# A gated attention and GLU kernel: output weight loads moved behind the h stores of their half, moments of tiles 8 to 11 split in two pairs

## The chip, the cores and the metric

The kernel runs on one core of a Trainium2 chip. The metric is the device time of one execution in microseconds (us); the time before is the median of three runs, 751.63 us (749.72 to 752.89). The five instruction streams are called PE (matrix products; its weight loads are PEld), DVE (vector), ACT (scalar), POOL (GpSimd) and SP (here it only issues DMAs). Each stream runs its instructions strictly in the order in which the program emitted them, and waits on semaphores for the others.

## The reference

With x of 2048 rows and 640 columns, everything in float32:

```
xn = layernorm(x)
q, k, v = split(xn @ wqkv)                  # 32 heads of 20 columns
attn = softmax over 8 keys, 2 rows apart    # pos, pos-2, ..., pos-14
s = (attn applied to v) @ wo
g = silu(((xn @ w_gate) * (xn @ w_up)) @ w_down)    # 1536 hidden columns
out = x + s * g
```

## The kernel before

The matrix products are made from float32 operands that are split in a high part (ACT copies the operand in a rounded form) and a low part (DVE or POOL subtracts the high part), and each product is the sum of three: high by high, high by low, low by high. `split(eng, raw, hi, lo)` is that pair of instructions (L109 on ACT, L110 on `eng`).

The 2048 rows are 16 tiles of 128. They are kept transposed in four chunks `xT[0..3]` of four tiles each, with a high and a low part. The hidden columns of the GLU are taken in 12 blocks f of 128.

**The beginning.** While PE multiplies the first tiles, the later ones are normalised and transposed. For tiles from 4 on, `moments_q(s, n)` takes mean and variance of n tiles on DVE (L255, L256: three instructions a tile); `load_xq` then overwrites the same buffers by DMA with the rows in another arrangement; `scales(s0)` computes the scale and shift of a whole chunk of four tiles, for tiles 8 to 15 with one instruction on ACT (L263), two on DVE (L266, L277) and seven on POOL (L278 to L334); `spread(s0)` multiplies these by a small matrix on PE (L340). `trans_q(s)` turns tile s: DVE first makes the low part of the tile before (`low_parts`, L370), then transposes (L365), then ACT makes the high part (L369). The low part of the last tile is therefore made at the next call of `low_parts`. `early_sums` are sums and differences of parts of chunks 0 and 1 on POOL (L593), which read chunk 1, tile 7 included, in both parts; the program emits three of them ahead of `scales(8)` and more behind it. `qkv(0, 0, i)` (L428) multiplies tile i; `gate_up(0, 1)` (L119) multiplies chunk 1, and `spread(8)` stands between its gate half and its up half.

**The long middle.** The projections and the GLU blocks run on PE, and the attention runs beside them on DVE and POOL as a generator, which the PE stages advance in small steps; `advance(1e9)` runs it to its end.

**The end of the GLU.** Blocks f = 3 to 10 are made by `group(f, 2)` and then `group(f, 0, 1)`, one half of the rows (two chunks) each. A half consists of seven products n = 0 to 6, whose kinds j come in the order 0, 5, 2, 1, 4, 3, 6 (L1327). They accumulate in three PSUM banks: A takes j = 0, 2, 4, 6, B takes j = 5 and C takes j = 1, 3. After j = 0, 2, 1 and 4 ACT copies the bank to SBUF (`hold`, L1294) into a buffer of the tag `gh`, which has five. As j = 6 accumulates into the same bank A as j = 4, it waits for that copy. `gate_a` (L1307), `gate_b` (L1297), `up_b` (L1300), `h_b` (L1303) and `up_a` (L1310) join the pieces on DVE or POOL; `up_a` and `h_b` each end with a DMA of 256 KB to `h_scr` on SP (L1283), and the buffer `kept[0]` or `kept[2]` comes free when that DMA has landed. `up_a` and `h_b` of a half are emitted in the first product of the next half. With the five buffers, the hold of j = 4 in the second half of f = 10 gets the buffer of `kept[0]` of its first half, and the hold of j = 4 of f = 11 that of `kept[0]` of the second half of f = 10.

A product's place can carry other work: `places[second, n]` for every block, and `beside[f, second, n]` for one block alone, emitted at the end of that product. Block f0 = 10 carries in this way the preparation of the output projection:

- `begin_last()`: ends the attention, loads the output weight `wo` with five DMAs of 320 KB on SP (L688), and reserves a tile.
- `load_pair(0)`: four DMAs of the attention's output (L704).
- `sums_wo()`: four sums of `wo` blocks on DVE (L936 to L939); the first reads the loads of k = 0 and 1, the second also those of k = 2 and 3.
- `split_wo(0, nc.vector)` and `split_wo(1, nc.vector)`: an ACT copy (L109) and a DVE subtraction (L110) each.

Behind block 10 come `group(f1)` for f1 = 11 (chunks 0 and 1), four plain products for chunks 2 and 3 (L119), and the output projection in pairs of tiles (L1033), whose operands `turn_pair` (L710, L982 to L985) and further splits of `wo` on POOL prepare.

Of the kernel before, what the change touches and what calls it, by code (L numbers as in the profile page):

```python
# [56 lines left out]
def kernel(  # L57
# [11 lines left out]
    nc = tc.nc  # L69
# [11 lines left out]
    def st(shape, tag, bufs, dt=F32):  # L81
        cnt[0] += 1
        return sb.tile(shape, dt, tag=tag, bufs=bufs, name=f"{tag}_{cnt[0]}")
# [39 lines left out]
    def slot(shape, dt=F32R):  # L123
        return st(shape, "s", SLOTS, dt)
# [85 lines left out]
    xc, xp, xs = st([P, 4, D], "kv", 2), st([P, 2, D], "pk", 1), slot([P, 2, D], F32)  # L210
# [38 lines left out]
    def moments(s0, n, mv=None):  # L249
        turns_few[0] += 1  # L250
        stats = part(few[:, 256 // 2 + turns_few[0] % 2 * 48:], [P, n, 2, 6])
        mv = st([P, n, 2], "mv", 3) if mv is None else mv
        for i in range(n):
            for a in range(2):
                nc.vector.bn_stats(stats[:, i, a, :], xt[s0 + i][:, a * HALF:(a + 1) * HALF])  # L255
            nc.vector.bn_aggr(mv[:, i, :], stats[:, i])  # L256
        return mv
# [62 lines left out]
    def moments_q(s, n):  # L320
        s0 = s // TPC * TPC
        moments(s, n, stat[s0][0][:, s - s0:s - s0 + n])

    def load_xq(s, n, t):
        nc.sync.dma_start(t, xq[:, s - TPC:s - TPC + n, :])
# [33 lines left out]
    def trans_q(s):  # L359
        apply_q(s)  # L360
        low_parts()
        if not turned:
            turned.append(slot([P, 2, KD, P], F32))
        y = turned[0][:, s % 2]
        nc.vector.transpose(y.rearrange("p k (q i) -> p k q i", i=QB),  # L365
                            xt[s].rearrange("p (q k j) -> p k q j", q=NQ, j=QB))
        hi, lo = xT_tile(s)
        apply_q(s + 1)
        nc.scalar.activation(hi, y, AF.Copy)  # L369
        halves.append(lambda: nc.vector.tensor_sub(lo, y, hi.bitcast(F32)))  # L370
# [49 lines left out]
    def qkv(m, r, i, runs=ALL_RUNS, at=None, act=None, bank=("q", 3)):  # L420

        c = MC[m]
        p = pt([P, 3 * c], *bank)
        t0 = (i % TPC) * P
        for n, (a, b, k) in enumerate(runs):
            if n == at:
                act()
            nc.tensor.matmul(p, xT[(r * NE + i) // TPC][a][:, k, t0:t0 + P], wq[m][b][k], start=n == 0,  # L428
                             stop=n == len(runs) - 1, skip_group_check=act is not None)
        if m or r:  # L430
            if not staged:
                y = slot([P, 2, 2 * 3 * CMAX], F32)
                staged.extend([y[:, 0], y[:, 1], st([P, 2 * 3 * CMAX], "pk", 1)])
            if c > CMAX and not wide:
                wide.extend([slot([P, 6 * c], F32), st([P, 6 * c], "pk", 1)])
            if i % 2 == 0:
                now[0] = wide if c > CMAX else staged
                now[0].insert(0, now[0].pop())
            n = len(MADE[m])
            y = now[0][0][:, :6 * c].rearrange("p (n a i c) -> p n a i c", n=n, a=3, i=2)  # L440
            nc.scalar.activation(y[:, :, :, i % 2, :].rearrange("p n a c -> p a n c"),
                                 p.rearrange("p (a n c) -> p a n c", a=3, n=n), AF.Copy)
            for k, g in enumerate(MADE[m]):
                if i % 2:
                    nc.scalar.dma_start(scr[2 * g + r][:, :, i - 1:i + 1, :], y[:, k])
                if i == NE - 1:
                    made.add(2 * g + r)
            if c > CMAX and (r, i) == (DIL - 1, NE - 1):
                staged.clear()
            return  # L450
        u = 0
        nc.scalar.activation(kv_t[u][:, :, W - 1 + i, :], p[:, c:].rearrange("p (a c) -> p a c", a=2), AF.Copy)
        nc.scalar.activation(q_t[u][:, i, :], p[:, :c], AF.Copy)
        for i0, i1 in ((1, 5), (5, NE)):
            if i == i1 - 1:
                for p0, p1 in ((0, 112), (112, 127)):
                    nc.sync.dma_start(kv_t[u][p0 + 1:p1 + 1, :, i0 - 1:i1 - 1, :],
                                      kv_t[u][p0:p1, :, W - 1 + i0:W - 1 + i1, :])
# [149 lines left out]
    def advance(budget):  # L608
        credit[0] += budget
        while running and credit[0] > 0:  # L610
            cost = next(running[0], 0)
            if cost == 0:
                running.pop()
            elif cost is None:
                break
            else:
                credit[0] -= cost
        if credit[0] > 0:
            credit[0] = 0
# [72 lines left out]
    def split_wo(k, eng=nc.gpsimd):  # L692
        y = slot([P, 2, D])
        hi, lo = y[:, 0], y[:, 1]
        split(eng, wo_raw.pop(k), hi, lo)
        wo_s[k] = hi, lo
# [233 lines left out]
    def sums_wo():  # L930

        r, u = wo_keep[:2]
        b11, b12, b21, b22 = r[:, :, :HALF], r[:, :, HALF:], u[:, :, :HALF], u[:, :, HALF:]
        t1, t2, t3 = (wo_sum[0][:, 2 * i:2 * i + 2] for i in range(3))
        t4 = st([P, KS, HALF], "o", 1)
        nc.vector.tensor_sub(t1, b12, b11)  # L936
        nc.vector.tensor_sub(t3, b22, b12)
        nc.vector.tensor_sub(t2, b22, t1)
        nc.vector.tensor_sub(t4, b21, t2)  # L939
        wo_keep.append({"T1": t1, "T3": t3, "T2": t2, "T4": t4})  # L940
# [26 lines left out]
    def load_pair(p):  # L967
        t = slot([P, 2, D], F32) if p == 2 else st([P, 2 if p else 5, D], "t" if p else "kv", 2)
        if not p:
            wo_sum.append(t[:, 2:].rearrange("p a (b c) -> p (a b) c", c=HALF))  # L970
            t = t[:, :2]
        load_o(2 * p, 2, t)
        t = t.rearrange("p a c -> p (a c)")
        pair_raw[p] = t[:, :3 * KS * P].rearrange("p (a c) -> p a c", c=P)
# [125 lines left out]
    gate_up(0, 0, part=part0)  # L1100
    gate_up(1, 0, early=(lambda: spread(4), lambda: trans_q(4), finish_piece, lambda: trans_q(5)))
    trans_q(6)
    trans_q(7)
    qkv(0, 0, 4)
    qkv(0, 0, 5)
    low_parts()
# [1 line left out]
    for _ in range(EARLY):  # L1108
        next(early)
    finish_piece()  # L1110
    moments_q(8, 4)
    load_xq(8, 2, xp)
    load_xq(10, 2, xs)
    scales(8)
    for _ in range(3):
        next(early)
# [46 lines left out]
    f0, f1 = KF - 2, KF - 1  # L1163
# [180 lines left out]
    beside = {}  # L1344
# [53 lines left out]
    for m, t in ((m, t) for m in range(1, len(MADE)) for t in range(DIL)):  # L1398
# [23 lines left out]
        elif (m, r) == (last, 1):  # L1422
            for k in range(2):
# [2 lines left out]
    w_split(2, "R")  # L1426
    w_sum.pop(2)
    load_wf(3)
    beside.update({(f0, 0, 5): lambda: begin_last(), (f0, 1, 1): lambda: (load_pair(0), sums_wo()),
                   (f0, 1, 2): lambda: split_wo(0, nc.vector), (f0, 1, 3): lambda: split_wo(1, nc.vector)})  # L1430

    def begin_last():
        advance(1e9)
        wo_keep.extend([load_wo((0, 1)), load_wo((2, 3)), load_wo((4,))[:, 0]])
        begin_wd("T4")
# [237 lines left out]
```

## Time and profile before

| | |
|---|---|
| median of three runs | 751.63 us (749.72 to 752.89) |
| the profiled execution, its own time | 751.81 us |
| its span, first to last instruction | 750.0 us |
| mean granted TensorE clock | 0.994 |
| PE busy | 737.2 us, 98% of the span |
| PEld, DVE, ACT, POOL busy | 670.5, 610.2, 302.1, 463.9 us |
| PE's share of the chain that ended last | 84% |

The profile is of one execution. A row of the timeline gives the start in us, the duration from the first start to the last end, the engine and line, the operation with its output and inputs, the number of merged instructions and, in brackets, how long the engine stood idle before it and who released it. Matmuls overlap a little, so the pace of PE is read from start to start. The chain of waits follows the work that ended last back from the end. The granted clock is 1.00 where TensorE runs at full speed.

### The profile page before, as it was taken

To read this page: it belongs to the slowest core of one execution; us is meant where nothing else is said; L and a number is where in the kernel's file an instruction comes from. 1 tells how busy PE (TensorE), PEld (TensorE's weight loads), DVE (VectorE), ACT (ScalarE), POOL (GpSimd) and SP (SyncE) were. 2 spreads that over 40 slices of the span, in tenths; PEclk is the share of its full clock that TensorE was granted. 3 is DMA by queue.
4 is the path that set the end of the run, shared out by engine and by line. 5 is a ranking of instruction groups with operands and counts; after the bars stand their busy time and mean duration, and the time that the engine had idled before them with its cause. 6 is when DMAs were issued, how large, how long until landed. Compare 5 with 4: busy or idle time off the path is not lost.

```text
span 750.0 us, 11103 instructions
## 1 busy us (share of the span) xinstructions
PE 737.2 (98%) x4054; PEld 670.5 (89%) x4054; DVE 610.2 (81%) x720; ACT 302.1 (40%) x577; POOL 463.9 (62%) x389
## 2 busy tenths in 40 slices
PE   8999999999999999999999999989999999999997
PEld 6989989988999998878887888868999999999997
DVE  7666998699797787998998998765998787777775
ACT  5658313322232332223322332235466564444442
POOL 6169929787788878788869889766659900000000
PEclk9999999999999999999999999989999999999999
DMA  9466663958447548937173514266667665555534
GB/s 326 158 196 218 234 209 98 287 158 249 129 135 223 180 128 240 282 120 219 43 200 106 151 44 118 64 182 178 173 186 214 211 235 190 190 190 190 190 106 140
DMA packets 103493, 132.97 MB, mean 177 GB/s; under 512 B 22697, under 2 KB 74405, under 8 KB 103439
## 3 DMA queue, kind: packets, MB, share of 16 engines
q1 hardware_dynamic: 84686, 112.77, 48.5%
q10 hardware_dynamic: 17600, 14.26, 5.8%
q0 software_dynamic: 1152, 5.24, 2.1%
q8 instruction: 31, 0.51, 0.3%
q14 instruction: 24, 0.19, 0.1%
HBM read 83.58 MB, written 47.81 MB: 175 GB/s over the span
## 4 chain that ended last, share of the span: by engine, by line
PE 84%; POOL 4%; DVE 4%; DMA 3%; ACT 2%; issue 2%; SPq 1%; POOLq 0%; ACTq 0%; DVEq 0%
PE g L1327 11%; PE q L428 9%; PE q L896 8%; PE u L428 8%; PE g L428 8%; PE u L1327 7%; PE u L896 6%; PE g L119 4%; PE u L119 4%; PE q L1327 3%; PE g L896 3%; PE e L896 3%; PE q L119 2%; DMA h_scr<-gh 2%; POOL o L504 2%
## 5 line engine op out<-in xcount | busy, mean ns | idle before, releaser
L504 POOL TENSOR_TENSOR o<-o,t 128x960 f32<-128x960 f32 (+1 forms) x69 | 139.8, 2026 | 19.0 <-DVE t L498 17.6
L498 DVE TENSOR_TENSOR t<-e,kv 128x960 f32<-128x960 f32 (+1 forms) x96 | 99.5, 1038 | 24.3 <-POOL o L504 24.2
L527 DVE TENSOR_TENSOR t<-q,kv 128x1920 f32<-128x1920 f32 (+1 forms) x48 | 92.4, 1926 | 5.3 <-DMA kv<-qkv_scr 5.2
L534 DVE TENSOR_REDUCE lg<-t 128x96 f32<-128x1920 f32 (+1 forms) x48 | 92.3, 1922 | 0.2
L110 POOL TENSOR_TENSOR s<-wraw,s 128x384 fp32r<-128x384 f32 (+6 forms) x58 | 70.1, 1220 | 23.4 <-ACT s L109 23.4
L428 PE MATMUL q<-s,xc 128*128 128x360 f32 (+1 forms) x450 | 82.7, 334 | 0.6 <-DVE lg L266 0.5
L1294 ACT ACTIVATE gh<-g 128x512 f32<-128x512 f32 x54 | 32.3, 598 | 122.3 <-PE g L1327 104.8
L428 PEld LDWEIGHTS q<-s,xc 128*128 128x128 f32 x450 | 74.9, 188 | 4.5 <-DVE lg L266 0.7
L428 PE MATMUL u<-s,xc 128*128 128x360 f32 (+1 forms) x360 | 65.8, 334 | 0.0
L428 PEld LDWEIGHTS u<-s,xc 128*128 128x128 f32 x360 | 60.3, 188 | 2.3
L428 PE MATMUL g<-s,xc 128*128 128x360 f32 (+1 forms) x330 | 61.5, 337 | 0.0
L428 PEld LDWEIGHTS g<-s,xc 128*128 128x128 f32 x330 | 55.7, 188 | 2.6
L1327 PE MATMUL u<-xc,s 128*128 128x512 f32 x216 | 55.6, 392 | 0.6 <-ACT gh L1294 0.3
L896 PE MATMUL q<-xc,s 128*128 128x320 f32 x342 | 55.5, 309 | 0.0
L1327 PE MATMUL g<-s,s 128*128 128x512 f32 x216 | 54.9, 390 | 0.0
L896 PEld LDWEIGHTS q<-xc,s 128*128 128x128 f32 x342 | 51.5, 188 | 0.0
L1327 PEld LDWEIGHTS u<-xc,s 128*128 128x128 f32 x216 | 40.3, 188 | 10.5 <-ACT gh L1294 1.5
L1327 PEld LDWEIGHTS g<-s,s 128*128 128x128 f32 x216 | 40.5, 188 | 8.5 <-ACT gh L1294 0.2
L1327 PE MATMUL g<-xc,s 128*128 128x512 f32 x168 | 43.6, 405 | 3.9 <-ACT gh L1294 3.9
L504 POOL TENSOR_TENSOR o<-t 128x960 f32<-128x960 f32 (+1 forms) x12 | 24.4, 2033 | 34.2 <-DVE t L498 27.1
L109 ACT ACTIVATE s<-wraw 128x384 fp32r<-128x384 f32 (+6 forms) x59 | 33.2, 586 | 28.7 <-PE g L1327 9.0
L1327 PEld LDWEIGHTS g<-xc,s 128*128 128x128 f32 x168 | 32.4, 195 | 12.2 <-ACT gh L1294 5.5
(367 smaller groups left out, 1574.0 us busy)
## 6 DMA issues: line engine op xcount, KB each, us to landing
h_scr<-gh SPq DMA_DIRECT2D x48, 256.0 KB, 2.5
wraw<-in_wgu SPq DMA_DIRECT2D x11, 640.0 KB, 4.4
kv<-qkv_scr SPq DMA_DIRECT2D x14, 480.0 KB, 6.1
qkv_scr<-s ACTq DMA_DIRECT2D x18, 360.0 KB, 3.8
t<-h_scr SPq DMA_DIRECT2D x8, 768.0 KB, 8.0
kv<-qkv_scr SPq DMA_DIRECT2D x14, 367.5 KB, 6.6
s_scr<-gh SPq DMA_DIRECT2D x16, 320.0 KB, 4.2
gh<-s_scr SPq DMA_DIRECT2D x16, 320.0 KB, 3.6
```

Source lines behind the costliest of these rows:

```text
L109: nc.scalar.activation(hi, raw, AF.Copy)
L110: eng.tensor_sub(lo, raw, hi.bitcast(F32))
L119: nc.tensor.matmul(acc, a, b, start=first and n == 0, stop=last and n == len(runs) - 1)
L428: nc.tensor.matmul(p, xT[(r * NE + i) // TPC][a][:, k, t0:t0 + P], wq[m][b][k], start=n == 0, stop=n == len(runs) - 1, skip_group_check=ac ...
L498: nc.vector.tensor_mul(t.rearrange("p (n d) -> p n d", d=DH), e[:, :, w].unsqueeze(2).to_broadcast([P, NE * nh, DH]), v)
L504: return NE * c * cost, lambda: eng.tensor_add(y, z, t)
L527: nc.vector.tensor_mul(t, q, k)
L534: nc.vector.tensor_reduce(out=lg[:, :, j:j + 2].rearrange("p n a -> p a n"), in_=t.rearrange("p a (n d) -> p a n d", d=DH), op=ALU.add, ax ...
L896: nc.tensor.matmul(p, y[:, i, k], wd_t[name][k][:, l], start=new and r == 0, stop=r == len(runs) - 1, skip_group_check=True)
L1294: nc.scalar.activation(kept[j], b["ACACABA"[j]], AF.Copy)
L1327: nc.tensor.matmul(y, w, x, start=j in (0, 1, 5) and r == 0, stop=r == len(runs) - 1, skip_group_check=True)
```

## The change

In the beginning, `moments_q(8, 4)` with its two loads is taken from behind `finish_piece()` and split: the moments of tiles 8 and 9 and their load come behind `trans_q(6)`, those of tiles 10 and 11 and their load behind `trans_q(7)`. `scales(8)` stays where it was. In block f0 the attention is still run to its end at place (0, 5); `begin_last` with the five weight loads goes to (1, 0), which is emitted behind `up_a` and `h_b` of the first half; `load_pair(0)` stays at (1, 1); the sums go from (1, 1) to (1, 4), the two splits from (1, 2) and (1, 3) to (1, 5) and (1, 6). `begin_last` calls `advance(1e9)` again, when the attention has ended.

```diff
     trans_q(6)
+    moments_q(8, 2)
+    load_xq(8, 2, xp)
     trans_q(7)
+    moments_q(10, 2)
+    load_xq(10, 2, xs)
     qkv(0, 0, 4)
     qkv(0, 0, 5)
     low_parts()
...
     finish_piece()
-    moments_q(8, 4)
-    load_xq(8, 2, xp)
-    load_xq(10, 2, xs)
     scales(8)
...
-    beside.update({(f0, 0, 5): lambda: begin_last(), (f0, 1, 1): lambda: (load_pair(0), sums_wo()),
-                   (f0, 1, 2): lambda: split_wo(0, nc.vector), (f0, 1, 3): lambda: split_wo(1, nc.vector)})
+    beside.update({(f0, 0, 5): lambda: advance(1e9), (f0, 1, 0): lambda: begin_last(), (f0, 1, 1): lambda: load_pair(0),
+                   (f0, 1, 4): lambda: sums_wo(), (f0, 1, 5): lambda: split_wo(0, nc.vector),
+                   (f0, 1, 6): lambda: split_wo(1, nc.vector)})
```

## The prediction

> **What bounds the kernel now.** I read the page first, then the chain of waits from 465 to 560 us, where the changed weight loads are issued.
>
> ```profile
> span 750.0 us, 11103 instructions
> PE 737.2 (98%) x4054; PEld 670.5 (89%) x4054; DVE 610.2 (81%) x720; ACT 302.1 (40%) x577; POOL 463.9 (62%) x389
> ```
>
> PE is busy for 98% of the span, so a change pays only where PE stands still or runs slowly, and costs where it makes PE do so. The chain shows such a place:
>
> ```profile
> 489.15 0.57 SPq L688
> ...
> 492.35 6.81 DMA h_scr<-gh
> ...
> 499.25 0.61 ACT gh L1294
> ```
>
> The first `wo` load is issued at 489.15; the store of `kept[0]` of the first half comes behind all five, at 492.35, and takes 6.81 us to land. Only then does ACT's hold of j = 4 get its buffer. The page gives the usual time of this store, and the timelines of PE, SP and DVE show what is held:
>
> ```profile
> h_scr<-gh SPq DMA_DIRECT2D x48, 256.0 KB, 2.5
> ```
> ```profile
> 482.49 2.20 PE L1327 MATMUL u<-xc,s 128*128 128x512 f32 x9
> 484.53 2.20 PE L1327 MATMUL g<-xc,s 128*128 128x512 f32 x9
> ...
> 487.93 2.20 PE L1327 MATMUL q<-xc,pk 128*128 128x512 f32 x9
> ...
> 494.74 2.21 PE L1327 MATMUL u<-xc,s 128*128 128x512 f32 x9
> 499.90 4.21 PE L1327 MATMUL g<-xc,s 128*128 128x512 f32 x9 [2.95 <-ACT gh L1294]
> ...
> 506.28 2.24 PE L1327 MATMUL q<-xc,pk 128*128 128x512 f32 x9
> ```
> ```profile
> 504.00:506.00 2.00, 2.00 (x6) 1.56 (x5) 2.00 (x4) 0.00 (x0) 2.00 (x3) 0.50 0.02 7
> ```
>
> In the first half j = 3 starts at 482.49 and j = 6 at 484.53, 2.04 later; in the second, j = 3 starts at 494.74 and j = 6 at 499.90 instead of 496.78. That is 3.12 us late. From the start of j = 6 to the start of j = 5 of the next group takes 487.93 - 484.53 = 3.40 us normally and 506.28 - 499.90 = 6.38 here: 2.98 us more, at a granted clock of 0.50 (the 0.50 near the end of the stretch row, ahead of the DMA share of 0.02). The place loses **6.10 us**.
>
> **The weight loads (gain).** The two stores now stand ahead of the five loads on SP.
>
> ```profile
> 489.19 0.68 DVE L1310 TENSOR_TENSOR gh<-gh,g 128x512 f32<-128x512 f32 x1
> 489.79 0.68 DVE L1303 TENSOR_TENSOR gh<-gh,gh 128x512 f32<-128x512 f32 x1
> 494.27 0.83 DVE L936 TENSOR_TENSOR kv<-t 128x640 f32<-128x640 f32 x1 [3.80 <-DMA t<-in_wo]
> 497.65 0.82 DVE L937 TENSOR_TENSOR kv<-t,t 128x640 f32<-128x640 f32 x1 [2.56 <-DMA t<-in_wo]
> ...
> 500.05 0.68 DVE L1307 TENSOR_TENSOR gh<-gh,q 128x512 f32<-128x512 f32 x1
> 500.64 3.18 DVE L110 TENSOR_TENSOR s<-t,s 128x640 fp32r<-128x640 f32 x2
> ...
> 504.35 0.67 DVE L1310 TENSOR_TENSOR gh<-gh,g 128x512 f32<-128x512 f32 x1
> ```
> ```profile
> 492.35 1.17 SPq L1283 DMA_DIRECT2D h_scr<-gh  x2
> ...
> 505.05 4.26 SPq L1283 DMA_DIRECT2D h_scr<-gh  x2
> ```
>
> `up_a` ends at 489.87, so its store goes out at about 489.9 and lands near 492.4 (2.5 us). The hold must start by 496.78 - 0.65 = 496.13 (0.65 is what lay between its start at 499.25 and PE's at 499.90). Even with the 6.81 us of now it would land at 496.7 and leave a wait of 0.6, too short to matter beside 3.12. I take the whole 6.10 as gained; the bounds are 5.5 and 6.10.
>
> **What the loads and sums do in their new place.** `h_b` ends at 490.47 and the two stores took 1.17 us to issue, so the first load goes out at about 491.06, 1.91 later than now. The second sum waits for the loads of k = 2 and 3, which landed at 497.65; they land between 497.65 (if bytes alone bound this stretch, the stores are merely served first) and 499.56. I take 499.0, nearer to the late end since the issue itself moves. DVE's queue behind it is then: three sums, the two splits, `gate_b`, `up_a`. `gate_a` is now emitted ahead of the sums and runs while DVE is idle. From L937 to the start of `up_a` it is 504.35 - 497.65 - 0.59 (the pitch of `gate_a`, 500.05 to 500.64) = 6.11 us, so `up_a` starts at 505.1 (503.8 to 505.7). Its store follows by 0.70 (505.05 - 504.35) and lands 2.5 later, at 508.3 (507.0 to 508.9). The hold of j = 4 in block 11 waits for exactly this buffer. A half is 494.74 - 482.49 = 12.25 us, so without the stall j = 3 of block 11 starts at 506.99 and j = 6 at 509.03; the hold must start by 508.38. It fits by 0.1 us, and misses by 0.5 at the late end: cost 0 to 0.5, I take **0.1**. The splits' ACT copies move behind the hold of j = 4 and wait for loads which have landed by then; behind them in ACT's queue stands the hold of j = 0 of block 11, which is not wanted before j = 2, more than 3 us into that block. `load_pair(0)` keeps its place behind the loads, and its reader `turn_pair(0)` stands on DVE behind `up_a`.
>
> **The clock.** That the idle time costs as much again in slow products is read from the rows above. The Trainium skill, page "TensorE: Matmul & The Clock Gate", section "Part 1: The HAM clock gate", says that the clock halves after an idle window of about 3.4 us and comes back after about 3.4 us of work. By it, an estimate: half of 3.4 us, 1.7 us, would be lost in place of 2.98, the gain would be 4.8 and the time 747.5. The trace differs: 2.95 us of idling was followed by some 6 us at half clock, and the measurement decides.
>
> **The moments (loss).** PE has a second wait, in the beginning:
>
> ```profile
> 39.72 4.96 PE L428 MATMUL q<-s,xc 128*128 128x360 f32 x30
> 44.52 3.56 PE L119 MATMUL g<-xc,s 128*128 128x512 f32 x15
> 49.11 0.41 PE L340 MATMUL e<-lg,lg 128*128 128x32 f32 x2 [1.04 <-POOL lg L334]
> ```
> ```profile
> 36.74 0.83 DVE L365 STREAM_TRANSPOSE s<-kv 128x640 f32<-128x640 f32 x1
> 38.75 0.83 DVE L370 TENSOR_TENSOR xc<-s,xc 128x640 fp32r<-128x640 f32 x1 [1.18 <-ACT xc L369]
> 39.49 0.84 DVE L365 STREAM_TRANSPOSE s<-kv 128x640 f32<-128x640 f32 x1
> 41.13 0.83 DVE L370 TENSOR_TENSOR xc<-s,xc 128x640 fp32r<-128x640 f32 x1 [0.80 <-ACT xc L369]
> 41.88 0.68 DVE L653 TENSOR_TENSOR gh<-u,gh 128x512 f32<-128x512 f32 x1
> 42.48 0.87 DVE L255 BATCH_NORM_STATS2 lg<-pk 128x6 f32<-128x320 f32 x2
> ...
> 44.51 0.83 DVE L255 BATCH_NORM_STATS2 lg<-s 128x6 f32<-128x320 f32 x2
> ```
> ```profile
> 40.37 0.74 ACT L369 ACTIVATE xc<-s 128x640 fp32r<-128x640 f32 x1 [1.65 <-DVE s L365]
> ```
> ```profile
> 42.04 2.54 POOL L593 TENSOR_TENSOR kv<-xc 128x512 f32<-128x512 f32 x2 [16.56 <-DVE xc L370]
> 44.53 1.29 POOL L593 TENSOR_TENSOR kv<-kv,xc 128x512 f32<-128x512 f32 x1
> 47.20 0.20 POOL L278 TENSOR_TENSOR lg<-lg 128x4 f32<-128x4 f32 x1 [1.37 <-DVE lg L277]
> ...
> 48.82 0.24 POOL L334 TENSOR_TENSOR lg<-mro,lg 128x32 f32<-128x32 f32 x1
> ```
>
> `spread(8)` waits 1.04 us for POOL's last instruction of `scales(8)`, which started when DVE had the moments. Taking the moments earlier would remove that wait, if POOL were free. It isn't: POOL's three early sums stand ahead, and they wait for the low part of tile 7, which is now behind all four moments on DVE. Two tiles of moments take 44.51 - 42.48 = 2.03 us. The transpose of tile 6 gives DVE free at 37.50 (pitch 0.75 to 0.77 from 41.13 to 41.88), the moments of 8 and 9 end at 39.53, the low part of tile 6 takes 0.74, the transpose of 7 starts at 40.27 (0.78 late) and ends its pitch at 41.04, the moments of 10 and 11 end at 43.07, and the low part of tile 7 starts there: 1.94 later than 41.13. POOL's sums then run from 43.98 to 47.76 (3.78 us, 42.04 to 45.82), and L278 starts there and not at 47.20: 0.56 late, and L334 and `spread(8)` with it. PE thus waits until 49.67: **+0.56**, with the bounds -1.04 (the wait gone) and +1.94 (the whole delay handed on). Tile 7's products start at 42.12 and want its high part, which shifts by 0.78 from 40.37, and from their eleventh on (43.72) the low part, ready at 43.9. Some 0.3 us are lost there at most, and they vanish in the wait before `spread(8)`: the gate half ends at 48.08 + 0.3. The two `load_xq` go out some 3 to 5 us earlier on SP; behind them wait DMAs of the first attention unit and one h store, which nobody wants for tens of us.
>
> **The sum** against the profiled execution: -6.10 + 0.1 + 0.56 = -5.44, a span of 744.6. Its own time, 751.81, is 0.18 above the median of the three runs, so I state it from the median: 751.63 - 5.44 = **746.2 us**.
>
> **Rivals.** *The wait moves one block on.* If DVE's sums end 0.5 to 2 us late, block 11's j = 6 stands as long: 746.6 to 748.1. For it speaks that my slack is 0.1 us; against it, that two DVE splits of 3.18 us overlapped with POOL splits in that row and may be shorter where POOL is done. *Not faster, then slower: the same mechanism past a point.* Place: the hold of j = 4 in block 11. If its wait reaches some 2.9 us, the clock falls again and adds 2.98: -6.10 + 0.56 + 2.9 + 2.98 is +0.3, or 752.0. That needs the loads of k = 2 and 3 at 501.8, 10.7 us behind the first issue at 491.06, where now they needed 8.5 (489.15 to 497.65). Slower by over 3.76 us needs a wait of 6.3 and these loads at 505.2, 14 us behind it. *The gain is given back by POOL.* The output projection's fourth product needs a low part of `wo` that POOL makes late:
>
> ```profile
> 528.99 1.75 POOL L110 TENSOR_TENSOR s<-t,s 128x640 fp32r<-128x640 f32 x1
> ```
> ```profile
> 533.68 1.04 PE L1033 MATMUL u<-s,xc 128*128 128x320 f32 x6
> ```
>
> POOL has it at 530.74 and PE wants it at about 534.1, its fourth matmul. Were POOL not to move, PE, 5.4 us earlier, would wait 2.0: 748.2. Against it: the splits ahead write tiles that come free with block 11's last product, so they move along with PE. *The moments help:* if the sums find POOL earlier than I order it, -1.04 in place of +0.56 gives 744.6.
>
> **Chances.** Forecast within half a us of its sum 0.62; the moments help 0.10; wait one block on 0.14; given back by POOL 0.06; clock falls again near 752 0.05; slower 0.03. A measurement of this kernel tells about 0.5% (3.76 us) from no change, so faster means under 747.87: the first two and about 0.09 of the third, 0.81; same 0.14 (the rest of the third, POOL, most of the clock case); slower 0.05, with a little of the clock case. The range goes from the moments' case, 0.2 below it for the runs' spread, to past POOL's case: 744.4 to 748.9, leaving out 0.08 above.
>
> **What would show it.** Right: no wait of PE on L1294 over 0.6 us between 480 and 512, granted clock 1.00 there, the store of `kept[0]` landing in about 2.5 us; in the beginning L340 near 49.7 with POOL's L593 starting near 44.0 and L278 following them without a gap. Wrong: PE idle before the j = 6 of block 11 or before the plain products, a clock of 0.50 in any stretch after 490, L340 at or before 48.4, or PE waiting on POOL's L110 in the projection.

## The result and the profile after

| | before | after |
|---|---|---|
| median | 751.19 us (11 runs, 748.69 to 752.89) | 748.88 us (11 runs, 747.81 to 749.68) |
| profiled execution, its own time | 751.81 us | 748.28 us |
| mean granted clock in it | 0.994 | 1.000 |

The ratio is 0.9969 (0.9956 to 0.9981): 2.31 us faster, where 5.44 less had been forecast. The page of the changed kernel:

```profile
span 746.5 us, 11102 instructions
PE 735.4 (99%) x4054; PEld 669.0 (90%) x4054; DVE 612.2 (82%) x720; ACT 302.5 (41%) x577; POOL 462.6 (62%) x389
```

Lines behind L1115 are one higher now: the hold is L1295, `gate_b` L1298, `up_b` L1301, `h_b` L1304, `up_a` L1311, the product L1328. PE's timeline of the changed kernel (start, duration, operation, in brackets the idle time before it and its releaser):

```profile
495.01 2.20 PE L1328 MATMUL u<-xc,s 128*128 128x512 f32 x9
497.05 2.20 PE L1328 MATMUL g<-xc,s 128*128 128x512 f32 x9
...
508.01 2.34 PE L1328 MATMUL u<-xc,s 128*128 128x512 f32 x9 [0.60 <-ACT gh L1295]
510.19 2.20 PE L1328 MATMUL g<-xc,s 128*128 128x512 f32 x9
...
525.83 1.04 PE L1033 MATMUL q<-s,kv 128*128 128x320 f32 x6
...
533.96 0.56 PE L1033 MATMUL e<-s,xc 128*128 128x320 f32 x2 [0.78 <-DVE xc L1012]
534.75 1.15 PE L1033 MATMUL q<-xc,kv 128*128 128x320 f32 x6 [0.23 <-DVE gh L1042]
...
537.30 1.14 PE L1033 MATMUL e<-xc,s 128*128 128x320 f32 x6
```

The stall of block 10 is gone: j = 6 starts 2.04 after j = 3 (497.05 - 495.01). Three small waits stand behind it. In block 11, j = 3 starts at 508.01, 13.00 behind the j = 3 of the half before, in place of the 12.24 of the half before that (482.77 to 495.01): 0.76 late. Behind this wait j = 3 itself takes 2.34 in place of 2.20, so that j = 6 is another 0.14 late, 0.90 in all. In the output projection PE waits 0.78 within the first product of the second pair, for a low part made by DVE (L1012), and 0.23 before the last product of the first pair, for DVE's L1042. The clock (ahead of the last two numbers) is full in the stretch that ran at 0.50 before:

```profile
504.00:506.00 2.00, 2.00 (x11) 1.65 (x10) 2.00 (x4) 0.60 (x1) 0.42 (x1) 1.00 0.04 8
```

SP's, DVE's, POOL's and ACT's timelines of the changed kernel show what stands behind the wait in block 11:

```profile
490.17 0.99 SPq L1284 DMA_DIRECT2D h_scr<-gh  x2
491.21 2.31 SPq L688 DMA_DIRECT2D t<-in_wo  x4
```
```profile
495.98 0.82 DVE L936 TENSOR_TENSOR kv<-t 128x640 f32<-128x640 f32 x1 [4.64 <-DMA t<-in_wo]
498.51 1.67 DVE L937 TENSOR_TENSOR kv<-t,t 128x640 f32<-128x640 f32 x1 [1.70 <-DMA t<-in_wo]
500.10 1.91 DVE L938 TENSOR_TENSOR kv<-t,kv 128x640 f32<-128x640 f32 x1
502.09 2.02 DVE L939 TENSOR_TENSOR o<-t,kv 128x640 f32<-128x640 f32 x1
...
504.77 0.68 DVE L1298 TENSOR_TENSOR gh<-gh,u 128x512 f32<-128x512 f32 x1
...
506.10 0.68 DVE L1311 TENSOR_TENSOR gh<-gh,g 128x512 f32<-128x512 f32 x1
```
```profile
496.62 2.88 POOL L110 TENSOR_TENSOR s<-wraw,s 128x768 fp32r<-128x768 f32 x2 [1.94 <-ACT s L109]
499.45 1.87 POOL L1301 TENSOR_TENSOR gh<-gh,gh 128x512 f32<-128x512 f32 x1
501.28 2.15 POOL L110 TENSOR_TENSOR s<-wraw,s 128x640 fp32r<-128x640 f32 x1
505.58 1.75 POOL L1304 TENSOR_TENSOR gh<-gh,gh 128x512 f32<-128x512 f32 x1 [2.15 <-issue]
```
```profile
507.36 0.60 ACT L1295 ACTIVATE gh<-u 128x512 f32<-128x512 f32 x1 [2.63 <-POOL gh L1304]
509.10 0.60 ACT L1295 ACTIVATE gh<-g 128x512 f32<-128x512 f32 x1 [1.14 <-DMA h_scr<-gh]
```

The two stores go out ahead of the loads, as intended. But the three sums that took 0.82 us each before (L937 to L939) take 1.67, 1.91 and 2.02. Each ends 0.7 us after the POOL instruction that was running: 500.18 after 499.50, 502.01 after 501.32, 504.11 after 503.43. POOL's L1301 in turn (1.29 us in block 11, at 509.86) ends 1.14 after L937 does. So the two engines alternate by whole instructions. `gate_b` and `up_a` start late; POOL's `h_b` needs `gate_b`, the hold of j = 1 (507.36) needs the buffer that `h_b` frees, and the hold of j = 4 (509.10) needs the one that the store of `up_a` frees. PE's j = 3 starts 0.65 behind the hold of j = 1 (507.36 to 508.01), so that is the hold that PE waits for. The hold of j = 4 would by the same 0.65 have let j = 6 start at 509.75, ahead of 510.05, where it stands 2.04 behind j = 3 in any case: in block 11 its lateness costs PE nothing, but it delays POOL, as the pairs show.

The same is seen in the pairs. From the first pair product to the third product of the second pair it takes 11.47 us (525.83 to 537.30); before it took 10.19:

```profile
530.80 1.04 PE L1033 MATMUL q<-s,kv 128*128 128x320 f32 x6
...
540.99 1.14 PE L1033 MATMUL e<-xc,s 128*128 128x320 f32 x6
```

That is 1.28 us given back. DVE's work of this stretch, before and then after, with POOL's beside it:

```profile
526.50 1.10 DVE L982 TENSOR_TENSOR t<-s 128x256 f32<-128x256 f32 x1
...
535.67 0.49 DVE L800 TENSOR_TENSOR lg<-wraw,lg 128x320 f32<-128x320 f32 x1
536.09 0.82 DVE L1012 TENSOR_TENSOR xc<-s,xc 128x640 fp32r<-128x640 f32 x1
```
```profile
518.91 3.81 POOL L110 TENSOR_TENSOR xc<-kv,xc 128x640 fp32r<-128x640 f32 x2
...
525.74 1.57 POOL L110 TENSOR_TENSOR xc<-kv,xc 128x640 fp32r<-128x640 f32 x1
```
```profile
521.53 1.85 DVE L982 TENSOR_TENSOR t<-s 128x256 f32<-128x256 f32 x1
...
531.43 1.05 DVE L800 TENSOR_TENSOR lg<-wraw,lg 128x320 f32<-128x320 f32 x1
532.41 1.50 DVE L1012 TENSOR_TENSOR xc<-s,xc 128x640 fp32r<-128x640 f32 x1
```
```profile
514.69 3.81 POOL L110 TENSOR_TENSOR xc<-kv,xc 128x640 fp32r<-128x640 f32 x2
...
521.53 1.56 POOL L110 TENSOR_TENSOR xc<-kv,xc 128x640 fp32r<-128x640 f32 x1
...
530.97 1.17 POOL L110 TENSOR_TENSOR xc<-wraw,xc 128x320 fp32r<-128x320 f32 x1 [2.00 <-ACT xc L109]
532.10 1.12 POOL L110 TENSOR_TENSOR kv<-wraw,kv 128x320 fp32r<-128x320 f32 x1
```

POOL's splits start 11.89 us ahead of the first pair product before and 11.14 after: 0.75 later against PE, because they stand on POOL behind `up_b` and `h_b` of block 11, and `up_b` waited for the late hold of j = 4. So L982 meets a POOL split at its start and not in its middle and takes 1.85 in place of 1.10, and everything behind it on DVE meets the next POOL splits (L800 +0.56, L1012 +0.68). Both L982 end 0.29 us after POOL's split does (527.60 after 527.31, 523.38 after 523.09).

By the Trainium skill, page "SBUF — State Buffer", section "SBUF: two separate sides", DVE with two SBUF inputs and a GpSimd instruction that reads SBUF contend for a shared port pair: it is an exclusive lock, and whichever starts first holds it for its whole instruction. The trace agrees, and also in what the rule leaves out: `up_a` (L1311), with one operand in PSUM, takes 0.68 us at 506.10 beside POOL's L1304, and `gate_b` (L1298) of the same shape takes 0.68 at 504.77, where POOL is idle.

In the beginning, PE's and POOL's timelines of the changed kernel:

```profile
49.46 0.41 PE L340 MATMUL e<-lg,lg 128*128 128x32 f32 x2 [1.03 <-POOL lg L334]
```
```profile
43.79 2.55 POOL L593 TENSOR_TENSOR kv<-xc 128x512 f32<-128x512 f32 x2 [17.92 <-DVE xc L370]
...
47.55 0.21 POOL L278 TENSOR_TENSOR lg<-lg 128x4 f32<-128x4 f32 x1
```

POOL's order is the forecast one, with L278 right behind the sums; `spread(8)` is 0.35 later than before (49.46 against 49.11), and the wait in front of it is unchanged. The delay is there in every profile that bears on it: from the start of the products of tiles 6 and 7 (L428) to `spread(8)` it takes 9.39 to 9.43 us in the four with the moments in their old place, and 9.73 to 9.76 in the thirteen with the moments moved and POOL's early sums left as they were.

### The profile page after: what moved, and what is told of

The parts are those of the page before. It is cut to its first block, busy times and chain, and to the rows that moved or that the text cites. A ratio compares the mean times of both kernels' runs of the same rounds, so it can differ in the third digit from the quotient of the medians.

```text
span 746.5 us, 11102 instructions
## 1 busy us (share of the span) xinstructions
PE 735.4 (99%) x4054; PEld 669.0 (90%) x4054; DVE 612.2 (82%) x720; ACT 302.5 (41%) x577; POOL 462.6 (62%) x389
## 5 line engine op out<-in xcount | busy, mean ns | idle before, releaser
L428 PE MATMUL q<-s,xc 128*128 128x360 f32 (+1 forms) x450 | 83.1, 334 | 0.6 <-DVE lg L266 0.5
L428 PEld LDWEIGHTS q<-s,xc 128*128 128x128 f32 x450 | 74.9, 188 | 4.8 <-DVE lg L266 0.8
L1295 ACT ACTIVATE gh<-g 128x512 f32<-128x512 f32 x54 | 32.2, 597 | 115.8 <-PE g L1328 97.8
L428 PE MATMUL u<-s,xc 128*128 128x360 f32 (+1 forms) x360 | 65.8, 334 | 0.0
L428 PEld LDWEIGHTS u<-s,xc 128*128 128x128 f32 x360 | 60.3, 188 | 2.3
L428 PE MATMUL g<-s,xc 128*128 128x360 f32 (+1 forms) x330 | 61.5, 337 | 0.0
L428 PEld LDWEIGHTS g<-s,xc 128*128 128x128 f32 x330 | 55.7, 188 | 2.6
L1328 PE MATMUL u<-xc,s 128*128 128x512 f32 x216 | 55.3, 391 | 0.9 <-ACT gh L1295 0.9
L1328 PE MATMUL g<-s,s 128*128 128x512 f32 x216 | 55.0, 390 | 0.0
L1328 PEld LDWEIGHTS u<-xc,s 128*128 128x128 f32 x216 | 40.3, 188 | 10.5 <-ACT gh L1295 2.0
L1328 PEld LDWEIGHTS g<-s,s 128*128 128x128 f32 x216 | 40.5, 188 | 8.6 <-ACT gh L1295 0.2
L1328 PE MATMUL g<-xc,s 128*128 128x512 f32 x168 | 41.5, 391 | 1.3 <-ACT gh L1295 1.3
L119 PE MATMUL g<-xc,s 128*128 128x512 f32 (+1 forms) x180 | 40.1, 373 | 0.0
```

The costliest lines, as they stand in the source:

```text
L119: nc.tensor.matmul(acc, a, b, start=first and n == 0, stop=last and n == len(runs) - 1)
L1295: nc.scalar.activation(kept[j], b["ACACABA"[j]], AF.Copy)
L1328: nc.tensor.matmul(y, w, x, start=j in (0, 1, 5) and r == 0, stop=r == len(runs) - 1, skip_group_check=True)
```

## The experiments

Times are medians; each ratio is to the kernel before on the same chip, with its 95% interval in brackets. Experiments start from the changed kernel unless said otherwise.

**The unchanged kernel once more**, for one further profile.

> A second profile of the kernel before, unchanged. My theory: the wait before j = 6 of block 10 is there again (2.4 to 3.1 us), and the half clock behind it differs from one execution to the next: j = 6 to the next j = 5 takes between 3.4 us (no fall) and 6.4 us. Rival: 6.4 us again, with the clock at 0.50, as in the first profile.

750.67 us at a mean granted clock of 0.997. PE's timeline and the windows (the granted clock stands ahead of the last two numbers):

```profile
482.80 2.20 PE L1327 MATMUL u<-xc,s 128*128 128x512 f32 x9
...
495.41 2.34 PE L1327 MATMUL u<-xc,s 128*128 128x512 f32 x9 [0.21 <-ACT gh L1294]
500.10 3.16 PE L1327 MATMUL g<-xc,s 128*128 128x512 f32 x9 [2.34 <-ACT gh L1294]
...
505.24 2.21 PE L1327 MATMUL q<-xc,pk 128*128 128x512 f32 x9
```
```profile
502.00:504.00 2.00, 2.00 (x6) 1.54 (x6) 2.00 (x2) 0.00 (x0) 2.00 (x2) 0.50 0.00 0
504.00:506.00 2.00, 2.00 (x9) 1.59 (x8) 2.00 (x4) 0.56 (x1) 2.00 (x3) 0.81 0.14 41
```

j = 6 comes 4.69 behind j = 3, 2.65 late, and the next j = 5 needs 5.14 in place of 3.40: 2.65 + 1.74 = 4.39 us lost, not 6.10. Here j = 3 itself is late as well, 12.61 behind the j = 3 of the half before in place of 12.24: another 0.37, for the hold of j = 1, which on ACT stands behind a `wo` split's copy. The stretch thus loses 4.76 in this execution. Of 159 executions of the kernel before, beside the experiments, the 18 with a mean granted clock of at most 0.995 have a median of 752.72, the 94 from 0.996 to 0.998 one of 751.00, and the 47 above one of 750.01. The first profile, at 0.994, belongs to the lowest group, and the second, at 0.997, to the middle one.

**One part of the change alone.** The moments alone (the loads and sums as before), then the loads and sums alone (the moments as before). The first undoes this part of the change; the second undoes the part in the beginning:

```diff
-    beside.update({(f0, 0, 5): lambda: advance(1e9), (f0, 1, 0): lambda: begin_last(), ...
+    beside.update({(f0, 0, 5): lambda: begin_last(), (f0, 1, 1): lambda: (load_pair(0), sums_wo()), ...
```

> Only the moments are moved; the weight loads stay as before. My theory: POOL's early sums wait for the low part of tile 7, so spread(8) comes at 49.4 to 49.5 instead of 49.11 and PE loses 0.35 us there; the stall before j = 6 of block 10 stays, and as its end is set by the attention it swallows most of that: span within 0.4 us of the kernel before, ratio 0.999 to 1.001. Rival (the moments help, the loss lies all in the loads): spread(8) before 48.5, about 1 us faster.

> Only the weight loads, sums and splits are moved; the moments stay as before. My theory: the stall before j = 6 of block 10 (3.1 us) and the half clock behind it are gone, 0.6 to 0.9 us come back as a wait of PE before j = 3 of block 11 and about 1.3 us in the first pairs of the output projection; the span of one profile is 3.5 to 4.2 us under the profile of before, the ratio 0.995 to 0.997, about 0.0005 under that of the whole change. Rival (the moments cost most of the missing gain): ratio under 0.994.

The moments alone: 751.28, 1.0006 (0.9993 to 1.0020). The loads alone: 749.20, 0.9985 (0.9973 to 0.9997), with waits of 1.00 in block 11 and 0.80 + 0.24 in the pairs. The gain is in the loads; the time of the moments can't be told from nothing.

**The change again**, beside the orders below.

> The changed kernel itself, as the measure for the runs beside it. My theory: the half clock behind the stall does not come in every execution of the kernel before (its executions lie between a mean clock of 0.994 and 1.000), so the change is worth the wait (some 3 us) and a part of the clock's 3 us, less 0.6 to 1.1 us before j = 3 of block 11, 1.0 us in the first pairs and 0.1 to 0.4 us at spread(8): 1.5 to 2.5 us, ratio 0.9965 to 0.998. Rival (the change gains the full 6.1 us and something else varies by chip): ratio under 0.993.

749.40, 0.9976 (0.9960 to 0.9993). Block 11 waits 1.14, the pairs 0.80 + 0.24. In this profile the first sum (L936), at 496.03, meets POOL too and takes 2.08 in place of 0.82, so that L937 starts 2.02 behind the j = 6 of block 10 (496.01 to 498.03) in place of 1.46 (497.05 to 498.51): 0.56 later, and the wait is 0.54 longer.

**The stores alone ahead.** From the kernel before: the stores of block 10's first half are issued by ACT, so that they pass the loads while loads and sums stay.

```diff
-        nc.sync.dma_start(h_scr[...
+        (nc.scalar if f == f0 and ch >= 2 else nc.sync).dma_start(h_scr[...
```

> The kernel before with one thing changed: the two h stores of the first half of block 10 are issued by ACT's queue and not behind the five loads on SP; loads, sums and splits stay where they were. My theory (the late loads and the sums that POOL slows are what gave part of the gain back): the stores land by about 494, no stall in block 10 and no half clock, the sums run at 494 to 500 as before, and the up_a of the second half starts at 504.4 instead of 506.1; the wait before j = 3 of block 11 is under 0.4 us; 1 us or more faster than the loads moved. Rival (the stores share the DMA engines with the loads and land as late as they did): hold of j = 4 at 498 or later and the stall stays.

753.03, 1.0036 (1.0021 to 1.0051): slower. PE's timeline:

```profile
495.90 2.34 PE L1327 MATMUL u<-xc,s 128*128 128x512 f32 x9 [0.43 <-ACT gh L1294]
...
504.90 3.15 PE L1327 MATMUL q<-xc,pk 128*128 128x512 f32 x9 [3.26 <-DVE gh L1307]
```

The old stall is gone, but now j = 5 of block 11 waits for `gate_a`, which stands on DVE behind the sums. The sums were expected to run as before; L937 to L939 take 2.25, 1.63 and 1.71 us in their old place, because POOL, no longer held up by the stall, now works beside them. The stall had covered a second late chain; taking only the first away uncovers it.

**The loads late, the sums and splits in their old place.**

```diff
-  ... (f0, 1, 1): lambda: load_pair(0), (f0, 1, 4): lambda: sums_wo(),
-      (f0, 1, 5): lambda: split_wo(0, nc.vector), (f0, 1, 6): ...
+  ... (f0, 1, 1): lambda: (load_pair(0), sums_wo()),
+      (f0, 1, 2): lambda: split_wo(0, nc.vector), (f0, 1, 3): ...
```

> The change with the sums and splits put back to (1, 1), (1, 2) and (1, 3), the loads left behind the stores. My theory: the ACT copy of split_wo(0) now waits for a load that lands at 496 and stands ahead of the hold of j = 1, so PE waits about 2.3 us before j = 3 of block 10; gate_a stands behind the sums on DVE until about 501 and holds j = 5 of block 11; 1 to 3 us slower than the change, about as slow as before. Rival (the place of the sums does not matter): same as the change.

751.93, 1.0015 (0.9997 to 1.0034). PE waits 1.41 before j = 3 of block 10 (ACT's copy for the split waits for its load ahead of the hold), 1.62 before j = 5 of block 11 (`gate_a` again), 0.19 before its j = 6, and 0.61 + 0.24 in the pairs. So the change's later place for the sums is a needed part of it.

**The sums behind `up_a`**, in the first product of block 11; then the same with the splits of `wo` on POOL.

```diff
-                   (f0, 1, 4): lambda: sums_wo(), (f0, 1, 5): lambda: split_wo(0, nc.vector), ...
-    beside.update({(f1, 0, 0): lambda: (turn_pair(0), load_pair(1)), ...
+    beside.update({(f1, 0, 0): lambda: (sums_wo(), split_wo(0, nc.vector), split_wo(1, nc.vector),
+                                        turn_pair(0), load_pair(1)), ...
```

> The change with the sums and both splits put one product further on DVE, behind gate_b and up_a (to the first product of block 11, ahead of turn_pair(0)). My theory: gate_b runs at 497 and up_a at 499.3, h_b comes free of DVE, and the wait before j = 3 of block 11 (0.6 to 1.1 us) goes; DVE's work is not less, so gate_b of block 11 is as late as now, POOL's splits too, and the 1.0 us in the first pairs stays or grows to 1.5: 0 to 0.8 us faster than the change. Rival (that wait comes from the store's landing and not from gate_b): the wait stays at 0.6 or more.

> As the kernel with the sums behind up_a, and the low parts of the two splits on POOL instead of DVE. My theory (DVE's lateness in block 11 is what makes the first pairs wait): DVE is done 1.5 us sooner, gate_b of block 11 runs before the block's last product ends, POOL's T1 split starts within 1.5 us behind it, and both the wait in block 11 and at least half of the 1.0 us in the pairs go: 1.2 to 1.8 us faster than the change. Rival (the pairs wait because POOL and DVE collide there anyway): the 1.0 us in the pairs stays, 0.5 to 0.9 faster.

749.47, 0.9981 (0.9965 to 0.9998), and 751.52, 1.0004 (0.9987 to 1.0021). Block 11 no longer waits, but the pairs wait 1.69 + 0.24 in both; on POOL the splits also held up the second plain product by 1.13. The sums still take 1.48, 2.21, 1.91 and 0.83: only the last ran without POOL.

**The sums behind the whole of block 11** (with it the two splits move to block 11's third product, two of POOL's splits of `wo` ahead of two others and of `gate`, and the second pair's loads to a buffer of their own); and the first pair's sums of `w_down` (L797, L800) behind `lo_pair(1, 0)`, in the change's order and with the sums behind `up_a`. The edit of the `w_down` sums:

```diff
-        if p < 3:
+        if 0 < p < 3:
             wd_sums()
...
-            if p == 3:
+            if p in (0, 3):
                 wd_sums()
```

> The change with the two splits put to the third product of block 11, the sums behind block 11 (where DVE stood idle from 515.5 to 519.3), POOL's splits of wo 4 and wo 2 ahead of T1 and T2, and the loads of pair 1 in a tile of their own. My theory (the sums delay DVE at a time when POOL holds the port they share): no wait before j = 3 of block 11, h_b of block 11 right at the block's end, the wait in the first pairs 0.4 us or less instead of 1.0: 1 to 1.7 us faster than the change. Rival (the pairs wait because of DVE's own work behind the plain products): wait in the pairs 1 us or more, gain under 0.8.

> The change with one thing more: in the first pair, the two sums of the first w_down block (L797, L800) are emitted behind lo_pair(1, 0) on DVE instead of ahead of it. My theory (the first pairs wait because DVE, slowed by POOL, comes late to lo_pair(1, 0)): DVE starts it 1.0 to 1.5 us sooner relative to PE, the wait in the first pairs falls from 1.0 us to 0.3 or less, the wait in block 11 stays at 0.6 to 1.1: about 0.7 us faster than the change, ratio 0.9965 to 0.9975. Rival (something other than DVE's queue holds that operand): the 1.0 us stays.

> The same with the sums and splits of wo behind up_a as well. My theory: no wait in block 11, and the wait in the pairs, 1.9 us with the sums there, falls by the same 1.0 to 1.5 us to 0.4 to 0.9; 0.7 to 1.4 us faster than the change. Rival (DVE's backlog only moves on to the next pair): the waits of PE between 500 and 560 us still sum to 1.8 us or more.

750.87, 1.0000 (0.9985 to 1.0015); 749.32, 0.9980 (0.9969 to 0.9991); 750.29, 0.9993 (0.9981 to 1.0005). The first waits 2.55 + 0.24 in the pairs; three of its sums take 2.18 or 2.19 us beside POOL's splits. In the second the wait on L1012 is gone and one of 1.33 on L1042 stands in its place, as L797 and L800 now meet POOL (1.17 and 1.05). The third waits 0.77, 1.17 and 0.16. Each of these orders of DVE's work only moved the wait.

**The early sums behind the scales** (from three ahead of them): six behind `scales(8)`, four behind it, and the four together with the sums behind block 11.

```diff
-EARLY = 3
+EARLY = 0
...
-    for _ in range(3):
+    for _ in range(6):
         next(early)
```

> The whole change, with all six early sums emitted behind scales(8) instead of three before and three behind. My theory: POOL reaches L278 at about 45.1 instead of 47.55, spread(8) needs no wait (about 48.3 instead of 49.46), PE gains 1.0 to 1.1 us over the whole change. Rival (DVE's order delays the scales anyway, or a later consumer of the sums waits): spread(8) stays at 49 or PE loses the same before 60 us; no gain.

> The whole change, with four early sums between scales(8) and scales(12), none ahead of scales(8) and the rest behind. My theory: POOL makes scales(8) at 45.1 to 47, the four sums until 52.1, scales(12) by 54.5; neither spread(8) nor spread(12) waits, and PE gains 1.0 us over the change, of which up to half may be taken back in the run-to-run waits between 320 and 400 us. Rival: one of the two spreads still waits 1 us.

> Both of the two kernels before it in this list together: 2 to 2.7 us faster than the change, ratio to the kernel before 0.993 to 0.995. Rival: the gains do not add, as one of them is taken back where the attention bounds PE: under 1.7 us.

749.11, 0.9983 (0.9972 to 0.9994); 751.48, 1.0006 (0.9991 to 1.0020); 751.57, 1.0005 (0.9990 to 1.0019). With six, `spread(8)` no longer waits but `spread(12)` does, for 1.16. With four neither does, but PE waits 2.03 at 90.48 for a copy on ACT (L441), which by the profile waits 8.84 us, in place of 3.88, for a store of what the early sums made (`t_scr`). In these orders the wait before `spread(8)` was moved, not removed.

**POOL away from the sums.** The low parts of block 11's weights S and R, and then of S, R and U, are made by DVE in place of POOL. That gives DVE more work and takes POOL's instructions from beside its sums.

```diff
-            split(nc.gpsimd, y, tw[to][:, 0, r], tw[to][:, 1, r])
+            split(nc.vector if f == f1 and t in "SRU" else nc.gpsimd, y, tw[to][:, 0, r], tw[to][:, 1, r])
```

> The change, with the low parts of block 11's weights S and R (768 and 384 columns) made by DVE instead of POOL; U stays on POOL. Theory (lock): where POOL and DVE both work on two operands in SBUF, each DVE instruction ends only 0.3 to 0.7 us after POOL's current one, so the four sums take 7.6 us in place of 3.3. With S and R on DVE, POOL starts near 498.9 with U; L937 runs alone, L938 or L939 still meets U or L1301. gate_b ends by about 504.3 (505.45 in the change), h_b by 506.1, hold of j = 1 of block 11 in time: wait in block 11 at most 0.3 (0.90 in all in the change). POOL's splits come 0.5 to 0.8 earlier against PE, L982 takes about 1.1 in place of 1.85, pairs wait at most 0.3 (1.01). Time 1 to 2 us under the change: ratio to the kernel before near 0.995. Rival (DVE's amount of work sets it): DVE gets 1.5 us more to do ahead of gate_b, so the waits in block 11 stay or grow to 1 to 2.4 us and the time is that of the change or above, ratio 0.997 to 0.999.

> The change, with the low parts of block 11's weights S, R and U all made by DVE instead of POOL, so that only up_b (L1301) of POOL runs beside the sums. Theory (lock): sums of 0.82 each but for one beside L1301; DVE's line from L936 to the end of the U split about 3.3 + 2.3 + one lock of 1.2; gate_b ends by 503.5 to 504.5, no wait in block 11, POOL 0.76 earlier against PE behind it, L982 at 1.1, pairs wait at most 0.3: 1.5 to 2.2 us under the change, ratio near 0.994 to 0.995. Rival (amount of work): 2.3 us more on DVE ahead of gate_b and up_a, block 11 waits 2 to 3 us, time above the change, ratio 0.999 or more, clock perhaps 0.50 behind the wait.

749.74, 0.9978 (0.9966 to 0.9991), and 749.60, 0.9980 (0.9964 to 0.9997). Both were expected at least 1 us below the change. With S, R and U on DVE the sums take 0.81, 0.81, 0.81 and 0.83 us, though DVE has more work. But S now waits for its ACT copy, at the head of DVE's queue (5.23 us idle, to 497.78), and `up_a` starts 8.31 behind the j = 6 of block 10, only 0.74 earlier than in the change (506.10 - 497.05 = 9.05); a split ahead of it still meets POOL's `h_b` and takes 1.92. With S and R alone block 11 does not wait, but the pairs do (1.70 + 0.23: POOL's `h_b` of block 11 came late); with all three the store of `up_a` landed late and block 11 waits 1.21, the pairs 0.56 + 0.24. That POOL's instructions are what lengthens the sums is shown; neither time is better than the change's.

**Both: the sums behind `up_a` and no POOL beside them.**

> Sums and wo splits behind up_a in the first product of block 11 (as in e5_sums_behind_up_a), and the low parts of block 11's S, R and U on DVE instead of POOL (as in e16), so that POOL is idle beside the sums. Theory (lock): sums 0.82 each, 3.3 us in place of 6.4 in e5; gate_b of block 11 runs at the end of its j = 3 or within 0.7 of it, POOL's h_b (L1304) and the splits behind it start as early against the pairs as in the kernel before (first split of 3.8 us about 11.9 us ahead of the first pair product, 9.9 in e5, 11.1 in the change); the pairs wait at most 0.4 us (1.93 in e5), block 11 not at all. Time 747 to 748, ratio near 0.9945 to 0.996. Rival (amount of work): with 2.3 us more work on DVE than e5 the pairs wait as long as in e5 or longer, or PE waits for gate_b or up_a of block 11; ratio 0.998 or more.

747.49, 0.9961 (0.9946 to 0.9977). DVE's timeline:

```profile
501.91 0.81 DVE L937 TENSOR_TENSOR kv<-t,t 128x640 f32<-128x640 f32 x1
502.64 0.82 DVE L938 TENSOR_TENSOR kv<-t,kv 128x640 f32<-128x640 f32 x1
503.50 0.82 DVE L939 TENSOR_TENSOR o<-t,kv 128x640 f32<-128x640 f32 x1
...
530.84 1.50 DVE L1012 TENSOR_TENSOR xc<-s,xc 128x640 fp32r<-128x640 f32 x1
...
533.06 1.66 DVE L1012 TENSOR_TENSOR s<-t,s 128x768 fp32r<-128x768 f32 x1
```

Block 11 does not wait, and the pairs' wait falls from the 1.93 of the order without this to 0.23, with 0.81 more behind it: two of DVE's low parts (L1012) still meet POOL's splits of `w_down`. The expected 0.4 was missed there. L937 to L939 run alone in both this run and the one with S, R and U on DVE, and in none of the runs that change only the order do all three; the interval of the time overlaps those of the change, so the time by itself doesn't tell them apart.

**Also no POOL beside the low parts of the second pair:** those three splits are emitted behind the last product of the first pair.

```diff
         pair_product(p, 4)
-        wd_splits()
+        if p:
+            wd_splits()
...
         pair_product(p, 6)
+        if p == 0:
+            wd_splits()
```

> e17_no_pool_beside_sums_behind_up_a, with the first pair's three POOL splits of w_down emitted behind the last product of that pair instead of behind its fifth, so that POOL is idle beside DVE's low parts (L1012) of the second pair. Theory (lock): the L1012 of 640 columns takes 0.81 (1.50 in e17) and the one of 768 takes 0.95 (1.66); L1042 starts 0.7 earlier and PE's wait of 0.23 for it goes, the wait of 0.81 for ACT's o L1036 behind L1044 shrinks to nothing; a collision may come back on the low parts of the third pair behind 537, of at most 0.7 us. From the first pair product to e<-xc,s x6 10.2 to 10.4 us (11.16 in e17). Time 0.3 to 1.0 us under e17's 747.5. Rival (the pairs' waits come from DVE's amount of work or from the evictions, not from POOL): the waits of 0.23 and 0.81 stay, time that of e17; or the delayed splits hold up ACT's high parts of the third pair and cost 0.5 us or more.

746.54, 0.9942 (0.9930 to 0.9955). DVE's and PE's timelines:

```profile
529.89 0.82 DVE L1012 TENSOR_TENSOR xc<-s,xc 128x640 fp32r<-128x640 f32 x1
...
531.42 0.95 DVE L1012 TENSOR_TENSOR s<-t,s 128x768 fp32r<-128x768 f32 x1
```
```profile
524.35 1.04 PE L1033 MATMUL q<-s,kv 128*128 128x320 f32 x6
...
534.11 1.15 PE L1033 MATMUL e<-xc,s 128*128 128x320 f32 x6
535.84 1.14 PE L1033 MATMUL u<-s,s 128*128 128x320 f32 x6 [0.58 <-ACT o L1036]
```

From the first pair product to the third of the second pair it takes 9.76 us (11.16 in the run before it, 11.47 in the change). One wait of 0.58 remains right behind that, where the delayed copies on ACT hold up an eviction: to the start of the next product it is 11.49, against 12.14 and 12.45, and 11.17 before the change. This is the best version found: its interval lies below that of the change, if only just (0.9955 against 0.9956, on other chips).

## Why the prediction was partly right

**What failed, in short.** Two things were mis-sized, and they make up the difference. The loss of the old stall, 6.10, was that of one execution; the next one shows 4.76 in the same stretch. And the durations of DVE's work were carried over from a place where POOL was idle: the term taken as 0.1 measured 0.90, and the pairs, taken at nothing, cost 1.28.

**Right.** The wait before the j = 6 of block 10 went, and its slow products with it; the stores went out ahead of the loads; the clock is 1.00 there; POOL's order in the beginning is the forecast one. The direction was right and the size less than half of the forecast. That the measured 748.88 still lies inside the range, 0.02 under its upper end, is luck: that end was drawn past the case of a late POOL split, which did not come. The forecast had put 0.81 on a time under 747.87.

**"I take the whole 6.10 as gained"**: the mechanism was right, the term was mis-sized. It was read from one execution, whose waiting and slow products were worth 6.10; the next one lost 4.39 in the same place, and 0.37 ahead of it. That the profile's clock of 0.994 was among the lowest could not be seen from it alone, and the sum was subtracted from the median of other executions. The clock rule cited from the Trainium skill, page "TensorE: Matmul & The Clock Gate", section "Part 1: The HAM clock gate", gave 1.7 us for the slow products; the second profile shows 1.74, the first 2.98, so that one trace had not decided it. The rule's idle window of about 3.4 us is not borne out: the clock fell behind shorter waits (last section).

**What the loads and sums do in their new place, "I take 0.1"**: 0.90. The step took 6.11 us from L937 to `up_a`; it is 7.59 (498.51 to 506.10). The loads were not the reason: they had landed by 498.51, ahead of the 499.0 assumed. The three sums had been taken at the 2.40 us that they needed before (497.65 to 500.05), and need 5.52 (498.51 to 504.03) beside POOL. Before, POOL was idle beside them because the stall held up the ACT copies that its splits wait for; the collision was in the old trace too, one step later, in the two DVE splits of 3.18 us, and these take 1.47 now. The duration of an instruction was carried over, but not the neighbour that it depended on. Also, only the buffer of j = 4 was priced; the wait that holds PE is that of j = 1, on `kept[1]`, which `h_b` frees behind `gate_b`. The rival "the wait moves one block on", held at 0.14, is thus what came, for the late sums that it names, but ahead of j = 3 and not of j = 6; the forecast took "POOL is done" there as an argument against it. With the sums at 0.81, when S, R and U were on DVE, the wait before j = 3 was gone.

**The pairs, at nothing**: 1.28 given back. The rival named a late POOL split for the fourth product, at 2.0 us if POOL didn't move. The argument against it was that the splits move along with PE. They did move, but 0.75 less than PE, and what became late was DVE's low part (L1012).

**The moments, +0.56**: right in mechanism, 0.35 in the traces; by itself not measurable in the time.

With the terms as measured, and 4.76 for the stretch of the stall, the account is -4.76 + 0.35 + 0.90 + 1.28 = -2.23. A second profile of the change has 1.44 in block 11 (13.54 in place of 12.24, and 0.14) and 1.30 in the pairs, which gives -1.67. The two comparisons of the change gave -2.31 and -1.46. With the first profile's 6.10, and the 0.28 by which the two profiled executions are apart at the j = 6 of block 10's first half (484.53 and 484.81), it gives -3.64, near the -3.53 between these two executions.

Left open: how often, over many executions, the place loses 4.76, 6.10 or something else is known from two profiles only. No run shows why a wait of a given length lowers the clock in one execution and not in another.

## What to carry to other kernels

Before a stall's whole cost is booked as gain, look for the chains that it covers, and size it over several executions where a clock falls behind it. When work is moved, the duration that it had in its old place is worth only as much as its neighbours: here a sum cost 0.82 us alone and up to 2.47 beside the other engine. Where reordering only moves a wait along, look for what lengthens the work, not for another order.

## What the runs showed of the hardware

- DVE with two operands in SBUF and POOL reading SBUF alternate by whole instructions: a DVE instruction of 640 columns ended 0.68 or 0.69 us after POOL's current one in three rows, one of 256 columns 0.29 us after it in two. With one operand in PSUM it took 0.68 us beside POOL and without it. The price is thus set by how much of the other's instruction is left, up to 1.65 us here (L938 at 2.47 in place of 0.82, with the sums in their old place and the loads late), and a shift of 0.75 us changed it by 0.75 (L982).
- A wait of PE was followed by a clock near 0.50 in some profiles (waits of 2.34, 2.95 and 3.26 us) and by none in others. Waits of the same length went both ways: 2.55 us in the pairs with full clock in the profile of the sums behind block 11, and with 0.50 where the four early sums were moved as well; 1.70 us in the pairs with 0.50 (538 to 540) in the profile with S and R on DVE, and 1.69 at the same place with full clock in the two with the sums behind `up_a`. Where it fell, it cost 1.74 and 2.98 us in two profiles of the same kernel.
